# Gated mix of 16-head attention and a spectral filter on one core: larger VectorE instructions, zero-column folds, and squares and small products moved between VectorE and GpSimd

## The chip, the cores and the metric

The kernel runs on one NeuronCore of a Trainium2 chip. The metric is the device time of one execution in microseconds (us). Instructions run on five in-order engines: TensorE (PE in the profile), ScalarE (ACT), VectorE (DVE), GpSimd (POOL) and SyncE (SP, which only issues DMAs). An engine works through its own instructions in the order in which they stand, and waits for the others through semaphores.

## The reference

One input `x` (2048 rows of 448, bf16) goes two ways, and a gate per row mixes them:

```
g = sigmoid((x * gate_w).sum(-1))
q, k, v = split(x @ wqkv, 16 heads of 28)
a = softmax(q @ k^T / sqrt(28)) @ v, heads joined, @ wo
b = irfft2(rfft2(x) * (w_r + 1j * w_i))          # over rows and columns
out = g * a + (1 - g) * b
```

## The kernel before

**Attention.** The heads go in 4 groups of 4 (`g`), the queries in 4 chunks of 512 (`qc`), so there are 16 chunks `c = 4 g + qc`. A chunk has 64 units of scores: 16 key tiles of 128 by 4 heads, each unit a matmul into 128 x 512 floats of PSUM (`scores`, L1143). A unit becomes weights in one of two ways. On ACT, an `exp` takes two units at once out of a two-bank buffer `psA` (L1166, 128 x 1024); there are two such buffers, and PE fills one while ACT reads the other. On DVE, a "z" step takes one unit out of a bank `psX` and builds the bits of the power of two by an integer addition (L1188, 128 x 512); it then needs two "shift" copies per pair of units (L1208, 128 x 1024 integers), on DVE or POOL, and PE multiplies three results with the values instead of one. PE adds up weights times values in one bank `psV` (`values`, L1227). At a chunk's end DVE copies `psV` to `Oraw` (L363, the helper `copy_to`), and a chain normalises it: row sums to DRAM and back, a reciprocal (L1283), the product with the gate's odds (`n4`, L1284, on DVE), a broadcast through DRAM, and a product on POOL (L1291).

**Projections.** Keys and queries of group g are projected (L351, the helper for all column-tiled matmuls), evicted by DVE (L533, L590) and squared into `sqk` on POOL (L544, L594) for their norms. Values are projected once for heads 0 to 3 in the head of the program, and for heads 4 to 15 in 16 pieces of 336 columns (`vproj`), each evicted by one DVE instruction (L363, `V<-psX`).

**The spectral branch** runs beside the attention. POOL folds `x` into sums and differences of columns d and 448-d (L720), leaving columns 0 and 224 to small copies (L722). PE applies the transforms; DVE evicts `AT` (L736) and `bufB` (L743). In the middle, for each of 16 groups of frequencies, PE makes the spectrum; DVE multiplies its 450 columns by the real and by the imaginary filter, one instruction each (L767, `T<-psX,Wst`); POOL combines them (L773, L775); PE transforms back, and DVE evicts two pieces of 113 and 112 rows (`vt_evict`, L816). At the end DVE evicts each of 16 row tiles (L800), and POOL unfolds it in three instructions (L805, L807, and L809 for two columns).

**Output.** For each of 16 row tiles t, PE adds four head groups times `wo` and the spectral part in one bank; DVE (L855) or, for the last four tiles, ACT (L857) scales it into one of four buffers `fin` (`fin_154` to `fin_157`, tile t into buffer t mod 4), and a DMA writes it out. Tile t waits until the DMA of tile t-4 has read the buffer. The last four tiles wait for the last chunk: `finale` (L1326) transposes, divides and transposes back `psV` in two halves on DVE (L1336 to L1345), after which PE adds each tile's last product.

**The order** of all this is not written by hand. Every step is an `Op` with a fixed cost per engine, and `plan()` runs a list scheduler over them before anything is emitted; the numbers in `TUNE` set due times and thresholds. `want_D` decides for each group of units how many take the DVE way, from the work it counts as waiting on DVE and POOL. Steps marked `port` are kept by the planner from running on DVE and POOL at the same time, and for shifts a dependency is added when the order is emitted, so that POOL's next step waits for DVE's:

```
if o.port and e == "DVE" and self.free_at["POOL"] > t + self.PW and t - o.at < self.PT:
    continue
...
if o.eng == "DVE" and o.kind == "shift":
    port = r
elif o.eng == "POOL" and port is not None and r is not None:
    self.tc.add_manual_dep(r.ins, port.ins.name, mybir.DependencyInfo(
        mybir.DependencyClass.Sync, mybir.DependencyReason.DATA), reason="common port")
```

Of the kernel before, what the change touches and what calls it, by code (L numbers as in the profile page):

```python
# [47 lines left out]
def constants():  # L48
    c = {}
    p = np.arange(128)  # L50
    small = np.zeros((128, 1152))
# [18 lines left out]
    small[:, 992:1120] = -C1.T  # L70
# [13 lines left out]
    for ch, (d0, lo) in enumerate(((0, 0), (HF - 1, 1), (1, 0), (HF - 2, 3))):  # L84
        dd = (d0 + np.arange(HF))[:, None]
        Bd[lo:HF, ch] = (np.cos if ch < 2 else lambda v: -np.sin(v))(2 * np.pi * dd * f / D)[lo:]
    c["Bd"] = Bd
# [6 lines left out]
    Bv = np.zeros((128, 2, D))  # L94
    for ch, (f0, fn) in enumerate(((0, 113), (113, 112))):
        Bv[:fn, ch, 0:F] = Br[f0:f0 + fn]
        Bv[:fn, ch, F:D] = Bi[f0:f0 + fn, 1:F - 1]
# [67 lines left out]
class Unit:  # L165
    __slots__ = ("bank",)

    def __init__(self):
# [3 lines left out]
TUNE = dict(T0=16487.535, LC=21704.657, late=6305.21, pzmin=4, urg=6, lastd=3, dt1=1190.3066700269546, dt2=962.0521051112778,  # L172
            minx2=1, poolt=4891.347115056346, th=141.972, pw=216.675, pt=2570.424, ph=426.68181980690866, slack=208.898,
            q0a=0.7, q0b=0.859, q0n=1.2209003708584167, v0=0.7381326711175313, v1=0.16, vr=0.293, kb=-3.0, ks=0.25, kn=-2.285,
            qb=-1.4867786877722318, qs=0.2435943825577399, qn=-1.89, gate=0.725, fo=1.497, fos=0.457, fa=4.071245811511132,
            fas=0.29, sp=3.653, sps=4811.435849142648, fc=7.428, fcs=0.272, fp=11.902, fps=0.165, fsd=46632.287,
            ow=12161.038102559343, ows=1062.607, u8=743.705, u12=13562.139, relx=10124.439740798462, comb=0, mc=28.681)
# [14 lines left out]
class Kernel:  # L192
    def __init__(self, tc, A_x, A_wqkv, A_wo, B_w_r, B_w_i, gate_w, out):
        self.tc = tc
        self.nc = tc.nc
        self.x, self.wqkv, self.wo = A_x, A_wqkv, A_wo
        self.w_r, self.w_i, self.gate_w = B_w_r, B_w_i, gate_w
        self.out = out
        self.ops = []
        self.NP = 24  # L200
        self.COMB = TUNE["comb"]

# [23 lines left out]
    def emit_all(self):  # L226

        port = None
        for o in sorted(self.order, key=lambda o: (o.start, o.num)):
# [3 lines left out]
            if o.eng == "DVE" and o.kind == "shift":  # L233
# [6 lines left out]
    def tiles(self):  # L240
# [4 lines left out]
        self.small = T([128, 1152], BF16, "small")  # L245
# [11 lines left out]
        self.Wv = self.Wst[0:112, 8 * D:12 * D].rearrange("p (c n) -> p c n", c=4)  # L257
# [6 lines left out]
        self.Bv = self.Bst[:, 0:2 * D].rearrange("p (c d) -> p c d", c=2)  # L264
# [9 lines left out]
        self.XF = vt[:, 0:NT * D].rearrange("p (t d) -> p t d", t=NT)  # L274
# [35 lines left out]
        self.C1N = self.small[:, 992:1120]  # L310
# [50 lines left out]
    def copy_to(self, eng, out, in_):  # L361
        if eng == "DVE":
            self.nc.vector.tensor_copy(out=out, in_=in_)  # L363
        elif eng == "POOL":
            self.nc.gpsimd.tensor_copy(out=out, in_=in_)
        else:
            self.nc.scalar.copy(out=out, in_=in_)  # L367

    def head(self):
# [3 lines left out]
        self.vd, self.kb_d, self.nq_d = [], {}, {}  # L373
# [6 lines left out]
        d_small = self.dma("small", lambda: dict(out=self.small[:], in_=self.cst["small"].ap()), 288, prio=H0 + 1.5)  # L380
# [13 lines left out]
        w_v = self.dma("Wv", lambda: dict(out=self.Wv, in_=wv[:, :, 2 * D:3 * D]), 400, prio=H0 + 6, rows=448)  # L394
# [42 lines left out]
        self.d_wv, self.d_gw = [w_v], d_gw  # L437
# [79 lines left out]
    def kproj(self, g, prio, prio_n, head):  # L517
# [3 lines left out]
        for b in range(4):  # L521
# [20 lines left out]
            else:  # L542
                e1 = self.ev(f"ke{g}{b}", {"DVE": 665.0}, fin, [p, self.d_f32] + old, pb, u=u)
                e2 = self.ev(f"ks{g}{b}", {"POOL": 1120.0}, lambda e, b=b: nc.gpsimd.tensor_tensor(  # L544
                    out=self.sqk[:, QW * b:QW * b + QW], in0=self.kT[g][:, QW * b:QW * b + QW],
                    in1=self.kT[g][:, QW * b:QW * b + QW], op=ALU.mult), [e1] + ([self.nq_d[g - 1]] if g else []), pb)
# [849 lines left out]
```

## Time and profile before

| | |
|---|---|
| three runs | 385.93, 385.90, 385.18 us (median 385.9) |
| profiled execution, its own time | 385.22 us |
| its span, first to last instruction | 383.4 us |
| busy in the span | PE 360.7, ACT 363.3, DVE 331.3, POOL 257.4 us |
| ACT's exps | 384 of 404 instructions, 353.8 us |
| DVE's z steps and shifts | 257 and 117 instructions, 171.0 and 49.8 us |
| granted TensorE clock | 0.999 |

In the profile a row reads: line, engine, operation, output<-input (partitions x elements, type) xcount | busy us, mean ns of one | idle time just before, and what ended it. Busy time is a union: where one instruction starts before the last has been reported ended, the mean times the count is more than the busy time. The span is 1.8 us shorter than the execution's time; what lies outside belongs to the start and end of a launch.

### The profile page before, as it was taken

The page shows a single profiled execution, that of the slowest core. Times are in us where ns is not written, and L with a number is a line of the kernel's source. Part 1 is how long each engine was busy: PE and PEld are TensorE (multiplying, and loading weights), DVE is VectorE, ACT ScalarE, POOL GpSimd, SP SyncE. Part 2 cuts the span into 40 slices and gives each one's busy share as a digit, 9 for nine tenths or more (in the row PEclk, how much of TensorE's full clock was granted, in tenths as well). Part 3 has the DMA queues.
Part 4 walks back from the last instruction along what each step waited for, and adds up shares of the span by engine and source line. Part 5 has one row for each costly group of instructions (what it writes and reads, how often), then busy time and mean ns, then how long its engine had stood idle before and what let it go on. Part 6 is the DMA issues. An engine that isn't in the chain of part 4 may idle for free.

```text
span 383.4 us, 13098 instructions
## 1 busy us (share of the span) xinstructions
PE 360.7 (94%) x5374; PEld 133.0 (35%) x5374; DVE 331.3 (86%) x636; ACT 363.3 (95%) x404; POOL 257.4 (67%) x292
## 2 busy tenths in 40 slices
PE   6999999999999999899999999999999989899994
PEld 5453233333233333333333433333333333232232
DVE  0567987986999999999999999999999899989962
ACT  3899999999999999999999999999999999999952
POOL 4327778778657676667757866667767666677692
PEclk9999999999999999999999999999999999999999
DMA  7700012201123312344122421312000000111012
GB/s 207 193 3 3 4 5 36 41 2 30 29 42 70 75 39 42 89 50 90 43 55 59 127 65 27 93 29 52 5 11 24 20 13 3 31 38 41 26 50 76
DMA packets 42869, 18.60 MB, mean 49 GB/s; under 512 B 28932, under 2 KB 40828, under 8 KB 42808
## 3 DMA queue, kind: packets, MB, share of 16 engines
q1 hardware_dynamic: 42808, 17.75, 21.1%
q8 instruction: 42, 0.69, 0.9%
q14 instruction: 19, 0.16, 0.2%
HBM read 13.77 MB, written 2.07 MB: 41 GB/s over the span
## 4 chain that ended last, share of the span: by engine, by line
PE 53%; ACT 29%; DVE 11%; issue 5%; DMA 2%; DVEq 0%; ACTq 0%
ACT P L1166 29%; PE psA L1143 19%; PE psX L351 16%; PE psV L1227 14%; DVE P L1188 5%; PE psX L403 1%; DMA out_dram<-fin 1%; DVE P L1208 1%; DVE AT L736 1%; PE psA L351 1%; PE psX L449 1%; DVE bufB L743 1%; PE psV L351 1%; DVE fin L855 1%; DVE bufB L800 0%
## 5 line engine op out<-in xcount | busy, mean ns | idle before, releaser
L1166 ACT ACTIVATE P<-psA 128x1024 bf16<-128x1024 f32 x384 | 353.8, 1139 | 1.3 <-PE psA L1143 0.7
L1208 POOL TENSOR_SCALAR P<-P 128x1024 int16<-128x1024 int16 x143 | 148.4, 1038 | 69.5 <-DVE P L1208 26.1
L1188 DVE TENSOR_SCALAR P<-psX 128x512 int16<-128x512 f32 x257 | 171.0, 683 | 17.3 <-PE psX L1143 14.6
L1143 PE MATMUL psA<-qT,kT 32*128 32x512 bf16 x767 | 149.0, 382 | 10.6 <-ACT P L1166 8.4
L1227 PE MATMUL psV<-P,V 128*32 128x512 bf16 x1538 | 132.7, 384 | 0.1
L1143 PE MATMUL psX<-qT,kT 32*128 32x512 bf16 x257 | 92.4, 385 | 0.0
L1143 PEld LDWEIGHTS <-kT 32*128 32x128 bf16 x1024 | 45.1, 91 | 134.9 <-issue 130.1
L1208 DVE TENSOR_SCALAR P<-P 128x1024 int16<-128x1024 int16 (+1 forms) x117 | 49.8, 429 | 0.5
L1227 PEld LDWEIGHTS <-V 128*32 128x32 bf16 x1538 | 33.3, 95 | 46.1 <-issue 41.7
L351 PE MATMUL psX<-xT,Wp 112*32 112x512 bf16 x512 | 40.4, 384 | 1.2 <-ACT Wp L367 1.2
L1291 POOL TENSOR_TENSOR qT<-Oraw,Rbc 128x512 bf16<-128x512 f32 x14 | 17.8, 1272 | 6.4 <-DVE P L1208 6.2
L594 POOL TENSOR_TENSOR sqk<-qT 128x512 bf16<-128x512 bf16 x14 | 14.5, 1039 | 6.3 <-DVE P L1208 5.9
L767 DVE TENSOR_TENSOR T<-psX,Wst 128x450 bf16<-128x450 f32 x32 | 18.7, 614 | 0.0
L351 PE MATMUL psX<-Wst,xT 112*32 112x336 bf16 (+1 forms) x384 | 16.9, 278 | 0.0
L720 POOL TENSOR_TENSOR VT<-bufA 128x892 bf16<-128x892 bf16 x8 | 14.2, 1776 | 2.7 <-DVE P L1208 2.5
L351 PEld LDWEIGHTS <-Wp 112*32 112x32 bf16 x512 | 10.2, 95 | 15.7 <-issue 13.6
L544 POOL TENSOR_TENSOR sqk<-kT 128x512 bf16<-128x512 bf16 x12 | 12.5, 1040 | 3.8 <-DVE P L1208 2.4
L351 PEld LDWEIGHTS <-VT 128*32 128x32 bf16 (+3 forms) x512 | 10.4, 95 | 10.2 <-issue 8.8
L773 POOL TENSOR_TENSOR bufA<-T 128x225 bf16<-128x225 bf16 x16 | 9.0, 560 | 6.5 <-DVE T L767 4.1
L816 DVE CAST VT<-psX 113x256 bf16<-113x256 f32 (+1 forms) x32 | 11.9, 414 | 0.5 <-PE psX L351 0.3
L351 PE MATMUL psX<-Bst,VT 113*32 113x225 bf16 (+3 forms) x256 | 11.7, 264 | 0.3 <-DVE VT L816 0.3
L805 POOL TENSOR_TENSOR bufA<-bufB 128x223 bf16<-128x223 bf16 x16 | 9.7, 609 | 3.4 <-DVE P L1208 3.2
(100 smaller groups left out, 290.0 us busy)
## 6 DMA issues: line engine op xcount, KB each, us to landing
Rbc<-dR SPq DMA_DIRECT2D x14, 256.0 KB
IV<-c_IV SPq DMA_DIRECT2D x16, 128.0 KB
bufA<-bufB SPq DMA_DIRECT2D x16, 112.5 KB
bufA<-in_A_x_dram SPq DMA_DIRECT2D x4, 448.0 KB
out_dram<-fin SPq DMA_DIRECT2D x16, 112.0 KB
S<-c_S SPq DMA_DIRECT2D x16, 96.0 KB
Wst<-in_B_w_r_dram SPq DMA_DIRECT2D x7, 112.5 KB
Wst<-in_B_w_i_dram SPq DMA_DIRECT2D x7, 112.5 KB
```

What stands on the lines that cost most here:

```text
L351: self.nc.tensor.matmul(o[c:c + n], lhsT=w[:, c:c + n], rhs=r, start=start, stop=stop, tile_position=(0, c), skip_group_check=True)
L544: e2 = self.ev(f"ks{g}{b}", {"POOL": 1120.0}, lambda e, b=b: nc.gpsimd.tensor_tensor(out=self.sqk[:, QW * b:QW * b + QW], in0=self.kT[g][: ...
L594: sq.append(self.ev(f"qs{g}{qc}", {"POOL": 1120.0}, lambda e, qc=qc: nc.gpsimd.tensor_tensor(out=self.sqk[:, QW * qc:QW * qc + QW], in0=se ...
L720: fs.append(self.ev(f"fo{tg}{k}", {"POOL": 1860.0}, lambda e, ts=ts, k=k, op=op, lo=lo, hi=hi: nc.gpsimd.tensor_tensor(out=self.XF[:, ts, ...
L767: es.append(self.ev(f"fm{g}{ri}", {"DVE": t_dve(F2)}, lambda e, u=u, T=T, g=g, ri=ri: nc.vector.tensor_tensor(out=T[:, ri, :].rearrange("p ...
L816: self.nc.vector.tensor_copy(out=self.VT[0:fn, ch, :, :, 8 * g:8 * g + 8], in_=u2.bank[0:fn, 256 * ch:256 * ch + 256].rearrange("p (r t k) ...
L1143: nc.tensor.matmul(out, lhsT=self.kT[g][32 * j:32 * j + 32, 128 * kt:128 * kt + 128], rhs=self.qT[g][qc][32 * j:32 * j + 32, :], start=Tru ...
L1166: e = self.op("exp", {"ACT": t_act(QW * n)}, lambda o: self.nc.scalar.activation(out=self.P[slot][:, 0:n, :], in_=self.PSA[i][:, 0:n, :], ...
L1188: e = self.op("z", {"DVE": t_dve(QW)}, lambda o: self.nc.vector.tensor_scalar(out=zt.bitcast(I16), in0=ub.bank, scalar1=float(ZBASE), scal ...
L1208: return en.tensor_scalar(out=self.P[q[1 + s]][:, 0:n, :].bitcast(I16), in0=self.P[q[0]][:, 0:n, :].bitcast(I16), scalar1=1.0, scalar2=flo ...
L1227: self.nc.tensor.matmul(self.PSV[32 * j:32 * j + 32, :], lhsT=self.V[:, kt, 4 * (i // NQ) + j, :], rhs=rhs, start=first, stop=False, tile_ ...
L1291: n = self.ev(f"n7_{c}", {"POOL": 1350.0}, lambda e: nc.gpsimd.tensor_tensor(out=self.qT[g][qc][:], in0=self.Oraw[r][:], in1=self.Rbc[r][: ...
```

## The change

The spectrum product becomes one instruction per group over 900 columns (both filters), and the middle eviction one of 512 columns over 113 rows (the second piece now begins one row earlier, at 112, with that row's weight zero). The values of heads 4 to 15 are projected in 4 pieces of 4 row tiles x 112 columns (heads 4 to 7) and 8 pieces of 2 row tiles x 224 columns (heads 8 to 15), whose weights are now loaded in two halves, the second into a free part of the tile `VT`. The fold works on 225 columns, with a zero column appended, so that its small copies go; the unfold loses its two-column copy in the same way. Squares may run on DVE or POOL; both shifts of a pair may run on either; `n4` goes to POOL. The ordering rule for `port` steps now covers every such step of DVE. All numbers in `TUNE` are new.

```diff
-            es = []
-            for ri in range(2):
-                es.append(self.ev(f"fm{g}{ri}", {"DVE": t_dve(F2)}, lambda ...: nc.vector.tensor_tensor(
-                    out=T[:, ri, :]..., in0=u.bank[:, 0:F2]..., in1=self.Wsp[:, g:g + 1, ri, :].to_broadcast([128, 2, F]), ...
+            e = self.ev(f"fm{g}", {"DVE": t_dve(2 * F2)}, lambda ...: nc.vector.tensor_tensor(
+                out=T[:].rearrange("p r (a f) -> p r a f", a=2),
+                in0=u.bank[:, 0:F2]....to_broadcast([128, 2, 2, F]),
+                in1=self.Wsp[:, g, :, :]....to_broadcast([128, 2, 2, F]), op=ALU.mult),
...
     def vt_evict(self, u2, g):
-        for ch, fn in ((0, 113), (1, 112)):
-            self.nc.vector.tensor_copy(
-                out=self.VT[0:fn, ch, :, :, 8 * g:8 * g + 8],
-                in_=u2.bank[0:fn, 256 * ch:256 * ch + 256]...)
+        self.nc.vector.tensor_copy(
+            out=self.VT[:, :, :, :, 8 * g:8 * g + 8].rearrange("p c r t k -> p (c r t) k"),
+            in_=u2.bank[0:HF, :].rearrange("p (m k) -> p m k", k=8))
...
+    def square(self, name, out, x, deps, prio):
+        o = self.ev(name, {"POOL": 1120.0, "DVE": 340.0}, lambda e: (self.nc.vector if e == "DVE" else self.nc.gpsimd).tensor_tensor(
+            out=out, in0=x, in1=x, op=ALU.mult), deps, prio)
+        o.port = True
...
-            so = self.op("shift", {"DVE": 70.0 + 0.265 * QW * n, "POOL": 110.0 + 1.05 * QW * n}
-                         if s == 0 else {"POOL": 110.0 + 1.05 * QW * n}, emit, prev, -1e7)
+            so = self.op("shift", {"DVE": 70.0 + 0.265 * QW * n, "POOL": 110.0 + 1.05 * QW * n}, emit, prev, -1e7)
...
-        r2 = self.ev(f"n4_{c}", {"DVE": 165.0}, lambda e: nc.vector.tensor_tensor(
+        r2 = self.ev(f"n4_{c}", {"POOL": 190.0}, lambda e: nc.gpsimd.tensor_tensor(
...
-            if o.eng == "DVE" and o.kind == "shift":
+            if o.eng == "DVE" and o.port:
...
-        for t in range(NT):
-            self.vproj(t, at(w["v0"] + w["v1"] * t), at(w["vr"] + 0.1 * t))
+        self.vd1 = [self.vproj(b, 4, ...) for b in range(4)]
+        self.vd2 = [self.vproj(b, 2, ...) for b in range(8)]
...
-            lo, hi = self.bufA[:, ts, 1:F - 1], self.bufA[:, ts, D - 1:F - 1:-1]
+            lo, hi = self.bufA[:, ts, 0:F], self.bufA[:, ts, D:F - 2:-1]
...
-TUNE = dict(..., poolt=4891.347115056346, ..., pt=2570.424, ..., v0=0.7381326711175313, ..., u8=743.705, u12=13562.139, ...)
+TUNE = dict(..., poolt=7236.982, ..., pt=5990.959, ..., v0=1.5, ..., va=4.36, ..., u8=-4013.039, u12=20639.587, ...)
```

The new order differs throughout. Counted over the whole of each engine's order, ACT has 383 exps of 1024 columns and one of 512 before, and 382 of 1024 now; DVE has 257 z steps, 117 shifts and no square before, and 260, 113 and 18 now; POOL has 143 shifts and 26 squares before, and 155 and 8 now; PE has 1538 matmuls of weights times values before, and 1544 now; its value projections for heads 4 to 15 are 256 matmuls of 336 columns before, and 256 of 112 and 256 of 224 columns now, each with a weight load. Three places follow.

DVE in the spectral middle: `T` is the spectrum product, `VT` the middle eviction, `P` from `psX` a z step, `P` from `P` a shift. Before:

```order
L767 TENSOR_TENSOR T_1_129<-psX_163,Wst 128x450 x2
L816 CAST VT<-psX_162 113x32x8
L816 CAST VT<-psX_162 112x32x8
L767 TENSOR_TENSOR T_0_128<-psX_161,Wst 128x450 x2
L816 CAST VT<-psX_163 113x32x8
L816 CAST VT<-psX_163 112x32x8
```

and now:

```order
L815 CAST VT<-psX_162 113x64x8
L1179 TENSOR_SCALAR P_103<-psX_161 128x512
L770 TENSOR_TENSOR T_0_128<-psX_163,Wst 128x900
L1179 TENSOR_SCALAR P_105<-psX_162 128x512
L1199 TENSOR_SCALAR P_96<-P_103 128x1024
L538 TENSOR_SCALAR kT_74<-psX_161,f32c 128x512
L1199 TENSOR_SCALAR P_100<-P_105 128x512
L368 TENSOR_TENSOR sqk<-kT_74 128x512
```

Four instructions per group have become two, they stand between z steps and no longer in one block, and a square of the keys has come in.

DVE at the end of the program: `psV` is read by the first transposes of `finale`, `fin` are the output tiles (here t = 9, 10, 11 in buffers 155, 156, 157). Before:

```order
L1336 STREAM_TRANSPOSE psX_162<-psV 128x256
L1338 RECIPROCAL Rsm_136<-psX_161 128x8
L1338 RECIPROCAL Rsm_137<-psX_162 128x8
L1340 TENSOR_TENSOR Rsm_136<-Rsm_136,oddsT 128x8
L855 TENSOR_SCALAR fin_155<-psA_159,omg 128x448
L1340 TENSOR_TENSOR Rsm_137<-Rsm_137,oddsT 128x8
L1342 TENSOR_TENSOR nq_92<-psX_161,Rsm_136 128x256
L1342 TENSOR_TENSOR nq_93<-psX_162,Rsm_137 128x256
L1345 STREAM_TRANSPOSE qT_3_90<-nq_92 128x256
L1345 STREAM_TRANSPOSE qT_3_90<-nq_93 128x256
L855 TENSOR_SCALAR fin_156<-psA_159,omg 128x448
L855 TENSOR_SCALAR fin_157<-psA_160,omg 128x448
```

and now:

```order
L846 TENSOR_SCALAR fin_155<-psX_161,omg 128x448
L1327 STREAM_TRANSPOSE psX_163<-psV 128x256
L1327 STREAM_TRANSPOSE psA_159<-psV 128x256
L1329 RECIPROCAL Rsm_136<-psX_163 128x8
L846 TENSOR_SCALAR fin_156<-psA_159,omg 128x448
L1329 RECIPROCAL Rsm_137<-psA_159 128x8
L1331 TENSOR_TENSOR Rsm_136<-Rsm_136,oddsT 128x8
L846 TENSOR_SCALAR fin_157<-psA_160,omg 128x448
L1331 TENSOR_TENSOR Rsm_137<-Rsm_137,oddsT 128x8
L1333 TENSOR_TENSOR nq_92<-psX_163,Rsm_136 128x256
L1333 TENSOR_TENSOR nq_93<-psA_159,Rsm_137 128x256
L1336 STREAM_TRANSPOSE qT_3_90<-nq_92 128x256
```

Tile 9 has moved ahead of the transposes, and tiles 10 and 11 from behind the whole chain into it. On PE, tile 9's products have moved ahead of the last multiplication with the values.

ACT at its end: the last exps, then output tiles 12 to 15. Before:

```order
L1166 ACTIVATE P_112<-psA_159 128x1024
L1166 ACTIVATE P_95<-psA_160 128x512
L857 ACTIVATE fin_154<-psA_160,omg 128x448
L857 ACTIVATE fin_155<-psX_163,omg 128x448
L857 ACTIVATE fin_156<-psA_159,omg 128x448
L857 ACTIVATE fin_157<-psA_159,omg 128x448
```

and now:

```order
L1157 ACTIVATE P_103<-psA_159 128x1024
L1157 ACTIVATE P_112<-psA_160 128x1024
L848 ACTIVATE fin_154<-psA_160,omg 128x448
L848 ACTIVATE fin_156<-psX_161,omg 128x448
L848 ACTIVATE fin_157<-psA_159,omg 128x448
```

The last exp is a whole one now, and tile 13 has gone to DVE.

160 lines of the change are left out of this document (74 added, 86 removed).

## Prediction

> **What bounds the kernel now.** I read the page's busy times and groups first, then busy times by stage, then the waits, and last the timeline of the end. From the page:
>
> ```profile
> PE 360.7 (94%) x5374; PEld 133.0 (35%) x5374; DVE 331.3 (86%) x636; ACT 363.3 (95%) x404; POOL 257.4 (67%) x292
> L1166 ACT ACTIVATE P<-psA 128x1024 bf16<-128x1024 f32 x384 | 353.8, 1139 | 1.3 <-PE psA L1143 0.7
> L1188 DVE TENSOR_SCALAR P<-psX 128x512 int16<-128x512 f32 x257 | 171.0, 683 | 17.3 <-PE psX L1143 14.6
> ```
>
> PE and ACT look alike at 94 and 95%. The second row tells them apart: ACT stood idle ahead of its 384 exps for 1.3 us in all. A matmul's reported time overlaps the next one's, so PE's share says less. An exp costs ACT 353.8 / 384 = 0.92 us (its reported 1139 ns overlaps the next). The busy times by stage, where the stages are the head, the first chunks, the middle, the last chunks, and what follows the last product with the values:
>
> ```profile
> 13.30:33.00 19.70, 19.11 (x492) 10.14 (x491) 12.53 (x22) 18.94 (x24) 7.61 (x12) 1.00 0.18 46
> 33.00:96.00 63.00, 63.00 (x864) 19.41 (x863) 50.89 (x97) 63.00 (x71) 49.35 (x45) 1.00 0.14 18
> 96.00:336.00 240.00, 228.95 (x3345) 82.01 (x3343) 231.97 (x451) 239.49 (x262) 164.30 (x180) 1.00 0.22 47
> 336.00:370.60 34.60, 33.53 (x440) 10.33 (x440) 28.53 (x53) 33.98 (x38) 25.87 (x36) 1.00 0.12 37
> 370.60:383.40 12.80, 7.14 (x138) 3.93 (x130) 5.15 (x14) 2.53 (x4) 5.81 (x15) 0.96 0.23 74
> ```
>
> The columns after the stage and its length are PE, its weight loads, DVE, ACT, POOL, the granted clock and the DMAs. From 33 to 370 us ACT is busy 336.5 of 337.6 us: the time of this stretch is the number of exps times 0.92. DVE has 8.0 us free of 240 in the middle, PE 11.0. The last stage is different: 12.8 us in which nobody is busy half the time except PE, a chain. In the timeline of its engines (start, length):
>
> ```profile
> 369.97 0.68 DVE L855 TENSOR_SCALAR fin<-psX,omg 128x448 bf16<-128x448 f32 x1 [0.95 <-PE psX L351]
> 370.64 0.80 DVE L1336 STREAM_TRANSPOSE psX<-psV 128x256 f32<-128x256 f32 x2
> 371.99 0.68 DVE L855 TENSOR_SCALAR fin<-psA,omg 128x448 bf16<-128x448 f32 x1
> 372.73 0.94 PE L351 MATMUL psA<-Wo,qT 128*32 128x448 bf16 x16 [0.84 <-DVE fin L855]
> 373.79 0.76 DVE L1345 STREAM_TRANSPOSE qT<-nq 128x256 bf16<-128x256 bf16 x2
> 374.48 0.64 DVE L855 TENSOR_SCALAR fin<-psA,omg 128x448 bf16<-128x448 f32 x1
> 375.29 0.68 DVE L855 TENSOR_SCALAR fin<-psA,omg 128x448 bf16<-128x448 f32 x1 [0.18 <-issue]
> 376.00 3.97 DMA out_dram<-fin
> 376.45 0.63 ACT L857 ACTIVATE fin<-psA,omg 128x448 bf16<-128x448 f32 x1 [6.46 <-PE psA L351]
> 377.40 0.63 ACT L857 ACTIVATE fin<-psX,omg 128x448 bf16<-128x448 f32 x1 [0.31 <-PE psX L351]
> 378.34 0.63 ACT L857 ACTIVATE fin<-psA,omg 128x448 bf16<-128x448 f32 x1 [0.31 <-PE psA L351]
> 379.03 0.37 PE L351 MATMUL psA<-Wo,qT 128*32 128x448 bf16 x4 [0.73 <-ACT fin L857]
> 380.06 0.63 ACT L857 ACTIVATE fin<-psA,omg 128x448 bf16<-128x448 f32 x1 [1.08 <-DMA out_dram<-fin]
> ```
>
> (The row of the DMA is from the chain that ended last.) The division of the last chunk ends at 374.55. But tile 11 is scaled only at 375.29, behind it; its buffer comes free 3.97 us later; tile 15, which uses that buffer, is scaled at 380.06 and is the end. PE, too, waited twice: 0.84 us for a bank that tile 9 held, 0.73 us for one that ACT held.
>
> **The change, part by part.** The sum is made against the profiled execution, 385.2 us, which stands 0.7 below the median of the runs, 385.9.
>
> *Exps.* Of the 1024 units, 260 instead of 257 take the DVE way. 764 units are 382 full exps, 767 were 383.5: 1.5 x 0.92 = **1.4 us less** on the engine that bounds 33 to 370 us. ACT's other steps are the same there and in the head.
>
> *DVE.* The rows by form, one with two neighbours for a price:
>
> ```profile
> L767 DVE TENSOR_TENSOR T<-psX,Wst 128x450 bf16<-128x450 f32 x32 | 18.7, 614 | 0.0
> L816 DVE CAST VT<-psX 113x256 bf16<-113x256 f32 (+1 forms) x32 | 11.9, 414 | 0.5 <-PE psX L351 0.3
> L736 DVE CAST AT<-psX 113x512 bf16<-113x512 f32 x16 | 10.8, 675 | 0.0
> L363 DVE CAST V<-psX 128x336 bf16<-128x336 f32 x16 | 8.0, 503 | 3.2 <-PE psX L351 3.2
> L363 DVE COPY xT<-psX 112x1024 bf16<-112x1024 bf16 x5 | 3.4, 687 | 8.9 <-PE psX L449 8.8
> L1284 DVE TENSOR_TENSOR Rsm<-Rsm,odds x14: 158/171/919, 62.0 to 339.9; 128x16 f32<-128x16 f32 x14
> L1284 DVE TENSOR_TENSOR Rsm<-Rsm,odds 128x16 f32<-128x16 f32 x14 | 5.6, 398 | 0.0
> L1208 DVE TENSOR_SCALAR P<-P x117: 284/417/695, 39.0 to 368.3; 128x1024 int16<-128x1024 int16 x114, 128x512 int16<-128x512 int16 x3
> L1311 DVE TENSOR_TENSOR nq<-Rbc,Rsm 128x512 bf16<-128x512 f32 x1 | 0.7, 691 | 0.0
> ```
>
> From 256 and 512 columns (414, 675 ns): 1.02 ns a column and 153 ns fixed. The product over 900 columns is then 1.07 us in place of 2 x 0.614, 16 times: -2.5. The eviction is 0.675 for 2 x 0.414: -2.45. The values: 12 x 0.61 for 16 x 0.503: -0.7. `n4` leaves: -5.6. Four shifts fewer at 0.43: -1.7; three z steps more: +2.05; tile 13: +0.7. The 18 squares, 512 bf16 columns with both inputs in SBUF, are not in the trace; the nearest rows are the shift (median 417 ns) and the product at 512 columns of floats (691). I take 417: the copy of 1024 bf16 columns costs 687, as 512 of floats do, so bf16 runs at twice the rate, and (675 - 153) / 2 + 153 = 414. +7.5, at most +12.4. Sum: 2.7 us less (2.2 more at the upper end), off the path while DVE's 8.0 us of idle time in the middle last. **0**.
>
> One rule speaks against the squares. The row of `n4` shows it first: the same instruction took 158 ns at best and 919 at worst. The Trainium skill says on its page GPSIMD Engine Reference, section 8, that POOL shares its SBUF interfaces with DVE, and that DVE instructions with two SBUF inputs contend with it. That would explain the 919, and a square has two such inputs. By the median rows the squares cost 7.5 us; if each waited as long as the worst `n4`, 18 x (0.691 + 0.748) = 25.9. I stay with the first, since the order keeps squares apart from POOL's steps as it does shifts, whose worst is 695; the second is a rival below.
>
> *POOL.* From
>
> ```profile
> L594 POOL TENSOR_TENSOR sqk<-qT 128x512 bf16<-128x512 bf16 x14 | 14.5, 1039 | 6.3 <-DVE P L1208 5.9
> L1208 POOL TENSOR_SCALAR P<-P 128x1024 int16<-128x1024 int16 x140 | 146.6, 1047 | 69.3 <-DVE P L1208 26.1 <-DVE P L1188 15.0 <-PE psX L1143 7.8
> L809 POOL COPY bufA<-bufB 128x2 bf16<-128x2 bf16 x16 | 3.1, 194 | 3.8 <-DVE P L1208 2.1 <-PE psX L351 0.8 <-PE psX L1143 0.4
> L722 POOL COPY VT<-bufA 128x8 bf16<-128x8 bf16 x4 | 0.9, 224 | 2.4 <-DVE P L1208 2.4
> L679 POOL CAST V<-wk 128x64 bf16<-128x64 f32 x1 | 0.5, 471 | 9.3 <-ACT wk L513 9.3
> ```
>
> 18 squares fewer (-18.7), 12 shifts more (+12.5), the small copies gone (-4.0 with those of the fold), 14 `n4` more at 0.19 to 0.47 each (+2.7 to +6.6). POOL gains 4 to 8 us of 257 and has 76 us free in the middle: **0**. `n4` now queues behind a shift, so up to 1.05 us later, and behind it SP's `dR` transfer with all that SP holds after that; the chain ends in a product that only the output reads, in the last group of heads. The added waits (POOL behind squares as behind shifts) cost POOL at most 18 x 0.8 (26.1 us over 33 waits now): 14 of its 76.
>
> *PE.* Six more products with the values, in sets of four, and value projections in twice as many instructions. The rows
>
> ```profile
> L351 PE MATMUL psX<-Wst,xT 112*32 112x336 bf16 x256 | 14.5, 310 | 0.0
> L351 PE MATMUL psX<-Wst,xT 112*32 112x112 bf16 x128 | 2.5, 213 | 0.0
> PE psA L1143 <- ACT P L1166: 8.4, 30, 0.5
> ```
>
> show 0.43 ns a column; 112 + 224 columns stream as long as 336. The 64 additional sets cost what is not per column: for 112 columns 2.5 us / 32 sets = 0.078, less 0.048: 0.03 each, 1.9 us; at the lower end nothing. It lies where PE waits for ACT (8.4 us). **0**, 1 to 2 if that cover is gone. The second half of the weights comes in one more DMA in the head, ahead of `Bd`, which nothing needs before the transforms. The first middle eviction now waits for the last value projection, as the order has it, just ahead of it on DVE; before, 16 of these evictions stood in a row without z steps between, and ACT was busy all the same.
>
> *The end.* Tile 9's scaling now stands ahead of the transposes: they start 0.6 us later. The chain from transposes to transposes took 370.64 to 374.55, 3.9 us, with one output tile in it; with two it is 4.6. So the division ends 0.6 + 0.1 + 4.6 = 5.3 us after the last product with the values, in place of 4.0. What follows is shorter. PE has 30 sets left in place of 35 and no bank to wait for; 22 of them (0.19 each, 4.2 us) are done before the division ends. Then one product (0.4 with its start), three ACT steps at the 0.95 us of the rows 376.45 to 378.34 (tile 13 goes beside them on DVE), so ACT ends at 5.3 + 0.5 + 2 x 0.95 + 0.63 = 8.3, or 7.7 if back to back. From ACT's end, 380.69, to the span's end are 2.7 us: 11.0 or 10.4 in place of 12.8. Tile 11 leaves DVE at about 3.9; even with 3.97 us of landing its buffer is free at 7.9, and the end at 11.2. So **2.0 us less**, between 1.6 and 2.4; 0 if the buffer or the chain holds it as now. That tile 9's five sets stand ahead of the last product hides behind the last two exps (1.8 us); without that it costs 1.0.
>
> 385.2 - 1.4 - 2.0 = 381.8. For a median I add a third of the 0.7 by which the profiled execution is low: **382.0**.
>
> **Rivals.** *The end gives nothing back* (a late output buffer, as now): 385.2 - 1.4 = 383.8. For it: the 3.97 us landing, which can fall on another tile. Against: three tiles now go out earlier. Chance 0.2.
>
> *PE holds ACT up where the values of heads 8 to 15 are now projected* (about 95 to 180 us). Two thirds of 64 x 0.145 = 9.3 us, 6.2, come into 85 us that have 11.0 / 240 of it free, 3.9: up to 2.3 late, 384.1, unless the transforms that start earlier make room. Chance 0.12.
>
> *DVE becomes the bound through the squares*, slower than before. DVE's 8.0 idle us and the 2.7 gained last until the squares cost 18.2 us, 1.0 each; every us beyond is a us of the kernel, and from 1.24 us each it is slower than before. At 1.44 each it is 7.7 over: 389.5. For it: POOL is busy 68% of the middle, and the 919 ns. Against: the median of 171 beside it. Chance 0.12.
>
> **How the numbers follow.** The forecast has 0.56. A run of this kernel can be told from no change beyond 0.2%, 0.8 us. Forecast, the first rival and most of the second lie below 385.1: 0.80, less what is unknown of stalls in a new order, 0.78. Slower: 0.16, the rest 0.06. The range goes from the end's best (2.4) with another us of luck, 380.4, to just short of no gain at all, 385.0; the third rival is left out.
>
> **What would show it.** Right: 382 exps at 0.92 us with little idle time ahead of them, squares near 0.42 us, the last ACT step 8 us after the last product with the values. Wrong: squares over 1 us, or exps that wait for PE between 95 and 180 us, or a last tile that waits for its buffer.

## Result and profile after

The changed kernel takes 382.25 us (median of 6, 380.70 to 383.48), the kernel before 385.55 (6, 385.13 to 385.93): ratio 0.9913, 95% interval 0.9888 to 0.9939. Forecast were 382.0 and faster. The sum came out; one of its two terms is hardly to be seen in the profile after, and the reason is worth more than the hit, which is in part luck (below).

The profiled execution of the changed kernel took 382.98 us, span 380.9. From the page, and from the groups by form:

```profile
PE 360.1 (95%) x5636; PEld 136.1 (36%) x5636; DVE 330.6 (87%) x604; ACT 360.5 (95%) x401; POOL 247.6 (65%) x281
L1157 ACT ACTIVATE P<-psA 128x1024 bf16<-128x1024 f32 x382 | 351.8, 1152 | 3.2 <-PE psX L1134 2.0 <-PE psA L1134 1.1
L770 DVE TENSOR_TENSOR T<-psX,Wst 128x900 bf16<-128x900 f32 x16 | 17.4, 1088 | 0.2 <-PE psX L350 0.2
L815 DVE CAST VT<-psX 113x512 bf16<-113x512 f32 x16 | 10.9, 680 | 1.9 <-PE psX L350 1.9
L362 DVE CAST V<-psX 128x448 bf16<-128x448 f32 x12 | 7.4, 618 | 0.5 <-PE psX L350 0.4
L368 DVE TENSOR_TENSOR sqk<-qT x10: 409/418/443, 43.3 to 269.8; 128x512 bf16<-128x512 bf16 x10
L368 DVE TENSOR_TENSOR sqk<-kT x8: 409/419/718, 52.1 to 236.1; 128x512 bf16<-128x512 bf16 x8
L1274 POOL TENSOR_TENSOR Rsm<-Rsm,odds x14: 215/216/217, 64.4 to 340.0; 128x16 f32<-128x16 f32 x14
```

382 exps, as counted; but ACT stood idle 3.2 us ahead of them where it was 1.3. The prices were right: product 1.088 us (1.07 forecast), eviction 0.680 (0.675), values 0.618 (0.61), squares 0.418 (0.417), `n4` on POOL 0.216 (0.19 to 0.47).

Cut where the exps begin and end, the two profiles differ so:

```
                                    before    after   difference
start to first exp                   13.48    12.94    -0.54
first exp's start to last one's end 356.50   356.37    -0.13
last exp's end to end of span        13.45    11.57    -1.88
```

The end gave what was forecast. The stretch of the exps, 1.5 of them shorter, did not move. Busy times of the changed kernel around its longest waits (columns as in the prediction, the granted clock third from the right):

```profile
300.00:302.00 2.00, 1.98 (x43) 0.75 (x33) 1.71 (x4) 2.00 (x4) 1.46 (x2) 1.00 0.29 81
302.00:304.00 2.00, 1.31 (x17) 0.45 (x13) 1.99 (x5) 2.00 (x4) 1.15 (x3) 1.00 0.15 58
304.00:306.00 2.00, 1.68 (x18) 0.58 (x17) 2.00 (x5) 2.00 (x3) 1.18 (x3) 1.00 0.00 0
306.00:308.00 2.00, 1.96 (x25) 0.71 (x26) 2.00 (x6) 2.00 (x3) 1.27 (x3) 0.58 0.03 8
308.00:310.00 2.00, 2.00 (x18) 0.24 (x10) 0.44 (x1) 1.13 (x2) 1.25 (x2) 0.50 0.14 4
310.00:312.00 2.00, 2.00 (x19) 0.44 (x17) 1.05 (x2) 1.40 (x2) 0.00 (x0) 0.50 0.00 0
312.00:314.00 2.00, 1.89 (x17) 0.38 (x13) 1.64 (x4) 1.63 (x2) 1.04 (x2) 0.71 0.00 0
```

From 306.3 to 313.1 us the granted clock is 0.5: PE is full and ACT waits. In the 4 us from 302 PE started 17 and 18 matmuls in 2 us, where it was 43 in the 2 us from 300. Not every execution has this: the mean clock of the six was 0.991, 0.994, 0.996, 0.999, 1.000 and 1.000. So below I also give means over the executions with a clock of 0.998 or more. Of the runs of before beside the experiments these are 42 of 57, and take 385.0 us. Of the 18 executions of the changed kernel and of two variants of it that have its order on PE and ACT up to 369 us they are 7, and take 381.3; the other 11 take 382.8. **The change is worth 3.7 us where the clock holds, and loses 1.5 of it in most executions.**

The end (timeline of its engines):

```profile
369.85 0.39 PE L1216 MATMUL psV<-P,V 128*32 128x512 bf16 x4
370.67 0.46 DVE L1327 STREAM_TRANSPOSE psX<-psV 128x256 f32<-128x256 f32 x1
371.81 0.68 DVE L846 TENSOR_SCALAR fin<-psA,omg 128x448 bf16<-128x448 f32 x1
372.62 0.68 DVE L846 TENSOR_SCALAR fin<-psA,omg 128x448 bf16<-128x448 f32 x1
373.35 0.56 PE L350 MATMUL psA<-Wo,qT 128*32 128x448 bf16 x8 [0.85 <-DVE fin L846]
373.96 0.76 DVE L1336 STREAM_TRANSPOSE qT<-nq 128x256 bf16<-128x256 bf16 x2
375.24 0.38 PE L350 MATMUL psA<-Wo,qT 128*32 128x448 bf16 x4
375.67 0.63 ACT L848 ACTIVATE fin<-psA,omg 128x448 bf16<-128x448 f32 x1 [6.36 <-PE psA L350]
377.13 0.63 ACT L848 ACTIVATE fin<-psA,omg 128x448 bf16<-128x448 f32 x1 [0.31 <-DMA out_dram<-fin]
```

Three ACT steps instead of four; the last ends 7.5 us after the last product with the values (370.24), where it was 10.1 (from 370.56 to 380.69).

### The profile page after: what moved, and what is told of

It reads as the page before. It is cut to its first block, busy times and chain, and to the rows that moved or that the text cites. A ratio compares the mean times of both kernels' runs of the same rounds, so it can differ in the third digit from the quotient of the medians.

```text
span 380.9 us, 13544 instructions
## 1 busy us (share of the span) xinstructions
PE 360.1 (95%) x5636; PEld 136.1 (36%) x5636; DVE 330.6 (87%) x604; ACT 360.5 (95%) x401; POOL 247.6 (65%) x281
## 4 chain that ended last, share of the span: by engine, by line
PE 60%; ACT 28%; DVE 5%; issue 4%; DMA 1%; ACTq 0%; DVEq 0%
ACT P L1157 27%; PE psA L1134 22%; PE psX L350 19%; PE psV L1216 16%; DVE P L1179 3%; PE psX L408 1%; DMA out_dram<-fin 1%; DVE P L1199 1%; PE psA L350 1%; ACT xT L365 1%; DVE VT L815 0%; DMA ident<-c_small 0%; PE psV L350 0%; PE psX L1134 0%; DVE T L770 0%
## 5 line engine op out<-in xcount | busy, mean ns | idle before, releaser
L1199 POOL TENSOR_SCALAR P<-P 128x1024 int16<-128x1024 int16 (+1 forms) x155 | 158.6, 1024 | 73.5 <-DVE P L1179 24.6
L1134 PE MATMUL psX<-qT,kT 32*128 32x512 bf16 x260 | 88.6, 387 | 0.0
L770 DVE TENSOR_TENSOR T<-psX,Wst 128x900 bf16<-128x900 f32 x16 | 17.4, 1088 | 0.2 <-PE psX L350 0.2
L350 PEld LDWEIGHTS <-Wp 112*32 112x32 bf16 x512 | 10.6, 94 | 15.7 <-issue 13.6
L350 PEld LDWEIGHTS <-xT 112*32 112x32 bf16 x768 | 12.8, 96 | 8.3 <-issue 7.3
L727 POOL TENSOR_TENSOR VT<-bufA 128x900 bf16<-128x900 bf16 x8 | 14.3, 1791 | 1.5 <-DVE P L1199 0.9
L350 PE MATMUL psX<-Wo,qT 128*32 128x448 bf16 x192 | 14.2, 356 | 0.0
L350 PEld LDWEIGHTS <-VT 113*32 113x32 bf16 (+2 forms) x512 | 9.9, 95 | 7.9 <-issue 6.8
L815 DVE CAST VT<-psX 113x512 bf16<-113x512 f32 x16 | 10.9, 680 | 1.9 <-PE psX L350 1.9
L778 POOL TENSOR_TENSOR bufA<-T 128x225 bf16<-128x225 bf16 x16 | 9.8, 613 | 4.1 <-DVE P L1199 4.0
L776 POOL TENSOR_TENSOR bufA<-T 128x225 bf16<-128x225 bf16 x16 | 9.0, 560 | 5.2 <-DVE P L1199 3.1
L846 DVE TENSOR_SCALAR fin<-psX,omg 128x448 bf16<-128x448 f32 x11 | 7.5, 678 | 5.1 <-PE psX L350 5.1
```

The source lines that it names most:

```text
L350: self.nc.tensor.matmul(o[c:c + n], lhsT=w[:, c:c + n], rhs=r, start=start, stop=stop, tile_position=(0, c), skip_group_check=True)
L727: fs.append(self.ev(f"fo{tg}{k}", {"POOL": 1860.0}, lambda e, ts=ts, k=k, op=op, lo=lo, hi=hi: nc.gpsimd.tensor_tensor(out=self.XF[:, ts, ...
L770: e = self.ev(f"fm{g}", {"DVE": t_dve(2 * F2)}, lambda e, u=u, T=T, g=g: nc.vector.tensor_tensor(out=T[:].rearrange("p r (a f) -> p r a f" ...
L778: y2 = self.ev(f"fz{g}", {"POOL": 580.0}, lambda e, T=T, g=g: nc.gpsimd.tensor_tensor(out=self.bufA[:, g, F:F2], in0=T[:, 1, 0:F], in1=T[: ...
L815: self.nc.vector.tensor_copy(out=self.VT[:, :, :, :, 8 * g:8 * g + 8].rearrange("p c r t k -> p (c r t) k"), in_=u2.bank[0:HF, :].rearrang ...
L1134: nc.tensor.matmul(out, lhsT=self.kT[g][32 * j:32 * j + 32, 128 * kt:128 * kt + 128], rhs=self.qT[g][qc][32 * j:32 * j + 32, :], start=Tru ...
```

## Experiments

In the tables and texts "idle" of 20 exps is the time from the first one's start to the 21st's, less 20 x 0.9045 us (the median between two starts is 0.904), worked out from their starts in the traces. (The 384 or 382 exps are cut at the same counts, so the columns of before and after stand for slightly different work. In the rows left out each variant lies within 0.21 us of the changed kernel.)

```
exps from   before  after  own   fill  fill1  sq2  sqpool  v2x
   0         3.25   3.85   5.74  3.77  4.36   3.74  3.96   3.77
  20         0.37   0.33   0.33  0.33  0.33   0.79  0.99   0.33
  40         0.23   0.26   0.26  0.26  0.26   1.67  1.84   0.26
 100         0.01   0.20   0.19  0.19  0.19   0.20  0.19   1.38
 120         0.35   0.35   0.36  0.36  0.36   0.35  0.36   0.82
 140         0.77   0.15   0.15  0.15  0.15   0.38  0.15   1.88
 160         0.40   0.36   0.35  0.35  0.36   0.76  0.94   1.24
 180         0.37   0.07   0.06   0.07   0.06   0.06  0.05   0.77
 220         0.50   0.27   0.27   0.27   0.27   0.76  0.27   0.27
 240         0.11   0.24   0.24  0.84  0.40   0.21  0.24   0.24
 300         0.37   2.60   0.38  0.77  0.55   0.38  0.38   0.39
```

**Output buffers (first rival).** In both kernels (before_own, after_own):

```diff
-        f = self.fin[t % 4]
+        f = self.bufB[:, t, 0:D]
```

> The kernel before, in which each output tile is scaled into its own slice of bufB (free by then) in place of one of four fin buffers; no instruction is moved. In the profile of before the last scaling on ACT began at 380.06 us after waiting 1.08 us for an output transfer, while its product, issued at 379.03, ended at 379.40. My reading: without that wait it begins about 0.2 us after the product, so the kernel gains 0.3 to 0.5 us: 385.1. The first rival (the end is set by late output buffers): the buffer accounts for the whole difference at the end, so 1.5 to 2 us: 383.6 to 384.0.

Measured 385.52 (12), 1.001 of before (0.9994 to 1.0026): nothing. ACT at the end of before_own:

```profile
376.98 0.64 ACT L857 ACTIVATE bufB<-psA,omg 128x448 bf16<-128x448 f32 x1 [6.94 <-PE psA L351]
380.02 0.64 ACT L857 ACTIVATE bufB<-psA,omg 128x448 bf16<-128x448 f32 x1 [0.52 <-PE psA L351]
```

From the first scaling on ACT to the last it is 3.04 us in place of 3.61: 0.57 is what the late buffer cost. The first comes 0.53 later, for in this variant a scaling on DVE waits 2.1 us for POOL steps on `bufB`; so the two cancel in the time. Either way the buffer does not make the 1.5 to 2 us of the rival.

> The changed kernel with the same edit, no instruction moved. In its profile the last scaling waited 0.31 us for an output transfer. My reading: 0 to 0.3 us less, 382.0 to 382.2; the first rival: 1 us or more, at most 381.2. All that runs before 369 us is the same program as the changed kernel, so this profile is also a second look at the stream of exps: by my count of 382 exps at 0.904 us each, it lasts about 355.2 us from the first exp's start to the last one's end where the granted clock stays at 1.0 (356.4 in the first profile, with a stretch of 6.8 us at 0.5); if the added steps cost the stream something everywhere, it lasts 356.4 again without such a stretch.

Measured 382.34 (6), 0.9926 of before (0.9904 to 0.9947), 381.4 in the three executions with full clock: no gain. The last scaling no longer waits for a transfer (0.17 us for PE instead of 0.31). Its profile has the half clock at another place, from 29.6 to 33.0 us, and not at 306: idle 5.74 in the first row of the table, 0.38 in the last. So the 2.2 us at 306 are not in the order, and without either stretch the exps last 356.09 - 1.97 = 354.1 us, less than the 355.2 that I expected; 356.37 - 2.2 gives 354.2 as well. Just ahead of that stretch PE was not short of matmuls, it started 182 in 4 us:

```profile
26.00:30.00 4.00, 3.33 (x182) 2.36 (x174) 1.94 (x6) 3.40 (x6) 0.03 (x1) 0.94 0.02 4
```

**Is the clock due to a sparse PE?** Products repeated into the same bank (after_fill; `num` counts the pairs of scores; after_fill1 repeats once):

```diff
+            more = 2 * mms[2:3] if 243 <= num <= 246 or 313 <= num <= 316 else []
-            for (c, kt, j), out in mms:
+            for (c, kt, j), out in mms + more:
```

> The changed kernel with 12 score products repeated into their own bank (two repeats each, the result is the same), at the six places near 240 and 303 us that have such a product and where TensorE had the fewest matmuls in 3.4 us (20 and 21 started, where the sparsest such stretch of before had 25). Theory: the stretch at a granted clock of 0.5 from 306 to 313 us follows from TensorE having little to do just before, and comes in some executions only. Then the mean granted clock is 0.999 or more in all runs (it was 0.991 to 1.000 in six of the changed kernel), the times lie within 1 us, and the median is 381.0 to 381.6. Rival: the clock falls whatever TensorE does there; then some runs show 0.99 again and the median is 382.0 to 382.7.

Measured 382.41, 0.9934 of before (0.992 to 0.9948). The clock was 0.998 to 1.000 in all six, the times 381.83 to 382.50. The theory's clock came, its median not: the repeats themselves hold the exps up, 0.6 us near 240 and 0.4 near 300 (table).

> The changed kernel with the score products near 240 and 303 us repeated once instead of twice (six repeats in place of twelve). Two repeats kept the granted clock at 0.998 and more in all six runs, but delayed exps: in 20 exps from 237 us the idle time ahead of them rose from 0.24 to 0.84 us, in those from 292 us from 0.39 to 0.77. One repeat should cost half of that, 0.5 us. If it is still enough to keep the clock up: all runs at 0.997 or more, 381.2 to 382.0. If it is not: some runs near 0.991 as in the changed kernel, and a median of 382.2 to 383.

Measured 381.16 (4, 380.85 to 382.14), 0.9889 of before (0.9865 to 0.9913), clock 0.998 to 1.000. The same place as above, in its profile:

```profile
304.00:306.00 2.00, 1.53 (x15) 0.43 (x14) 1.81 (x5) 2.00 (x4) 1.15 (x2) 1.00 0.07 28
306.00:308.00 2.00, 1.85 (x28) 0.62 (x22) 2.00 (x6) 1.93 (x3) 1.15 (x2) 1.00 0.02 4
308.00:310.00 2.00, 1.92 (x32) 0.62 (x24) 2.00 (x5) 2.00 (x4) 1.55 (x2) 1.00 0.01 4
```

Ten of ten executions with repeats stayed at 0.998 or more, 7 of 18 without them. That is weaker evidence than it looks: of the four other variants below that keep the sparse places (sq2, sqpool, v2x, l3) 27 of 41 executions stayed there with no repeats, and the repeats stand nowhere near the stretch at 29.6 us. The 2 us from 304 are even sparser here than where the clock fell; what exactly is counted stays open. This is the lowest median measured, but its interval overlaps the changed kernel's: beyond its steady clock no gain is shown.

**The larger instructions alone** (after_split): product and eviction issued as two instructions each, at the same places.

```diff
-                out=T[:]..., in0=...to_broadcast([128, 2, 2, F]), ...
+                out=T[:, ri, :]..., in0=u.bank[:, 0:F2]..., ... for ri in range(2)
...
+        for ch in range(2):
+            ...tensor_copy(out=self.VT[:, ch, :, :, 8 * g:8 * g + 8], in_=u2.bank[0:HF, 256 * ch:256 * ch + 256]...)
```

> The changed kernel with the spectrum product again as two instructions of 450 columns and the middle eviction again as two of 256 columns; what runs before and after them on each engine is unchanged. By the rows of before and after this is 16 x (2 x 0.614 - 1.088) = 2.2 us and 16 x (2 x 0.414 - 0.680) = 2.4 us more on DVE, which idles 26 us of the 335 from 33 to 368 us. My theory (DVE does not set the time; its larger instructions buy nothing by themselves): 0 to 0.5 us more than the changed kernel, 382.3 to 382.9. Rival (the larger instructions on DVE are where the gain is from): 2 to 4.6 us more, 384.3 to 387.

Measured 382.52, 0.9927 of before (0.9903 to 0.9952). Its profile has the half clock at 306.1 to 312.9 as well, and the exps last 356.46 us beside 356.37. The split cost nothing. It was a smaller dose than I expected, though: DVE's busy time rose from 330.6 to 332.6 us, by 1.9 and not by 4.6, since neighbouring instructions overlap by some 0.08 us, which the rows' means count twice.

**Squares.** Twice on DVE (after_sq2), or all 18 on POOL (after_sqpool), the order otherwise unchanged:

```diff
+ after_sq2:    the same tensor_tensor issued for i in range(2 if e == "DVE" else 1)
+ after_sqpool: lambda e: self.nc.gpsimd.tensor_tensor(out=out, in0=x, in1=x, op=ALU.mult)
+               if o.eng == "DVE" and o.port and o.kind != "sq":     # no POOL step waits for a square on DVE
```

> The changed kernel with each of the 18 squares issued twice on DVE, no other instruction moved: 18 x 0.41 = 7.4 us more on DVE, and POOL's next step waits behind the second square as well. My theory: most of it falls into DVE's idle time, so 0 to 1.5 us more than the changed kernel, 382.3 to 383.8. The third rival of the prediction (DVE is close to the bound, and two-input steps in SBUF hold POOL up): 4 to 7.4 us more, 386.3 to 389.7.

> The changed kernel with its 18 squares issued on POOL, at the same places of the order: DVE has 7.4 us less, POOL 18.7 us more. By the prediction's ledger POOL has some 76 us free there and DVE is off the path, so the engine does not matter: 382.0 to 382.6. Rival, from doubled squares (7.4 us more on DVE cost 2 to 3 us, most of it between 34 and 70 us where POOL's shifts waited for them): what counts is how long POOL's shifts stand behind a square, 1.04 us in place of 0.41, so 1 to 4 us more than the changed kernel, 383.3 to 386.3.

Measured 384.44 (12 runs, 0.9992 of before, 0.9974 to 1.001) and 384.55 (11 runs, 0.9979, 0.9963 to 0.9995); at full clock 384.3 and 384.3 beside 381.3: **3.0 us each**. So in this order the squares' place on DVE is worth most of the change's 3.7. My number for the first was too low, the third rival's too high; for the second the rival was right, and the ledger wrong. Busy times of the changed kernel, of after_sq2 and of after_sqpool, in this order, for the stretch of the first squares:

```profile
34.00:75.00 41.00, 40.68 (x714) 14.35 (x710) 38.88 (x73) 41.00 (x48) 30.28 (x26) 1.00 0.19 25
```

```profile
34.00:75.00 41.00, 40.12 (x677) 13.66 (x673) 39.41 (x75) 39.94 (x45) 29.18 (x25) 1.00 0.18 22
```

```profile
34.00:75.00 41.00, 39.50 (x644) 13.34 (x643) 38.56 (x66) 39.50 (x45) 34.22 (x31) 1.00 0.17 20
```

ACT loses 1.1 and 1.5 us there while DVE and POOL both have time left: 1.6 and 11.8 us free with doubled squares. So it is not the sum of an engine's work. I read it as a queue: a shift stands behind a square for 0.4 us more, or 0.6 where POOL does the square, and the products with the values behind the shift. POOL's waits that a square ended rose from 6.6 us in the changed kernel to 13.1 with doubled squares, which bears out the first half; the profiles name no wait of PE for a shift, so the second is argued. The square itself stays at its price in the median, 424 ns even when doubled.

The squares that took longer, up to 0.718 us in the changed kernel and 0.893 doubled, show what holds them. One of them, with the POOL step beside it:

```profile
51.48 1.04 POOL L1199 TENSOR_SCALAR P<-P 128x1024 int16<-128x1024 int16 x1 [1.21 <-PE psX L1134]
52.07 0.72 DVE L368 TENSOR_TENSOR sqk<-kT 128x512 bf16<-128x512 bf16 x1
```

The shift on POOL ends at 52.52, the square 0.27 later. It is so in every such case (ns, by the time that POOL was busy beside the DVE step; those between 100 and 150 ns left out):

```
                                 under 100 ns       150 ns or more
                                 count, length      count, length, length less POOL's time beside it
square, changed kernel and sq2   45, 408 to 427       7, 443 to 893, 269 to 282
shift, before                    89, 363 to 430      15, 440 to 695, 278 to 284
n4, before                        5, 158 to 166       6, 258 to 919,  19 to 31
z step, before                   14, 673 to 692     241, 628 to 693, no constant
```

The three steps that read SBUF alone end a fixed time after the POOL instruction beside them; the z step, which reads PSUM, takes as long either way. The squares are cheap since the order, in which POOL waits behind them, leaves 15 of the 18 under 100 ns beside POOL. What they cost without that ordering rule was not tried.

**PE's cover (second rival)** (after_v2x): the value projections of heads 8 to 15 computed twice.

```diff
+        for k in range(3, 8, 4) if n == 2 else ():
+            mms[k] = (..., lambda fs=[...the four products again...]: [f() for f in fs])
```

> The changed kernel in which the value projections of heads 8 to 15 are computed twice, the second time into the same bank with the same result: 256 more matmul instructions on PE (64 sets of four) between 109 and 187 us, no other engine's work changed. A set costs PE 224 x 0.43 / 1000 + 0.03 = 0.126 us at my rates, 8 us in all; PE has 1.3 us left in which it waits for nothing from 95 to 180 us in the profile of the changed kernel (3.95 in before). Theory (the second rival's cover was real, and the change has used it up to the last 1.3 us): the exps now wait for PE there, and the kernel takes 4 to 7 us more, 386 to 389. Rival (PE's busy time overstates its load, the cover is larger): 0 to 2 us more, 382.3 to 384.3.

Measured 385.91 (12), 1.0035 of before (1.0009 to 1.006), just below my 386 to 389; 385.8 at full clock, 4.4 more than the changed kernel. From 104 to 208 us, first the changed kernel, then this one:

```profile
104.00:208.00 104.00, 101.43 (x1574) 37.55 (x1566) 96.87 (x174) 104.00 (x115) 74.41 (x80) 1.00 0.30 58
```

```profile
104.00:208.00 104.00, 101.99 (x1769) 40.45 (x1766) 93.57 (x165) 101.01 (x109) 71.67 (x76) 1.00 0.29 57
```

ACT is busy all 104 us in the changed kernel; here it loses 3. The table has the loss in the rows from 100 to 180 (5.0 us) and nowhere else. The second rival named a real limit; the change stopped short of it. Of the 8 us that I reckoned for the doubling 4.4 came through, so by these rates some 3.6 us of cover were left and not 1.3.

**What an exp costs** (after_noz8): no unit of chunk 8 goes the DVE way.

```diff
-        if len(us) < n + 3 or us[-1][0] != c or (c == NQ * NG - 1 and kt >= NK - self.LASTD):
+        if len(us) < n + 3 or us[-1][0] != c or (c == NQ * NG - 1 and kt >= NK - self.LASTD) or c == 8:
```

> The changed kernel in which no unit of chunk 8 goes the DVE way: 387 full exps and a half instead of 382, 11 z steps fewer on DVE, and the order after chunk 7 planned anew. My theory (between 33 and 369 us each exp costs its 0.904 us): 5.5 x 0.904 = 5.0 us more than the changed kernel, 387.3, within 1 us for the new order. Rival (the time is set as much by DVE, PE and the waits between them, so exps for z steps is an even trade): 0 to 2 us more, 382.3 to 384.3.

Three executions with a clock of 0.995 to 0.997 took 388.0, 389.4 and 389.6 (1.0097 of before, 1.0065 to 1.0128); the other four, at 0.951 to 0.970, 395.9 to 400.0. So 6.7 us or more above the changed kernel's 381.3, in place of 5.0. The profile (an execution of 400.0 us) shows where the rest lies:

```profile
208.00:240.00 32.00, 31.40 (x252) 7.03 (x251) 14.48 (x22) 24.77 (x26) 9.52 (x13) 0.52 0.19 49
```

For 30.7 us the clock stayed at 0.5 although PE was busy 31.4 of the 32, and ACT was idle for 7 of them. In the three groups of 20 exps that hold its stretches at half clock (from 200, 220 and 340) the idle time is 11.7 us more than in after_own. Without these the exps last 370.8 - 11.7 = 359.1 us, 5.0 more than 354.1: the price of an exp is right. The end is not the same here: from the last product with the values to the end of the span it is 12.5 us in place of 10.6. These 1.9 us, from the order planned anew, and the 5.0 account for the 6.7 of the fastest execution, which at a clock of 0.997 has no room for a stretch of 3.41 us at half clock.

**The end's order** (after_l3): `lastd=3`.

> The changed kernel with lastd = 3 in place of 2: no unit of the last three key tiles of the last chunk goes the DVE way. The order differs from the changed kernel's only at the very end: half an exp more, two output tiles instead of one scaled ahead of the transposes, one instead of two within the division, and all partial sums of the last four tiles stand ahead of the division's end, with their last products together behind it. My reading: +0.46 us of exps, the last scaling 0.8 us earlier after the last product with the values: 381.9. If the exps alone counted: 382.7. If a tile ahead of the transposes costs its 0.6 us in full and nothing comes back: 383.3.

Measured 382.57, 0.9944 of before (0.9925 to 0.9962), 382.3 at full clock: 0.9 more than the changed kernel. Half an exp is 0.45; the end is 11.2 us from the last product with the values (368.51) in place of 10.6. (The median is close to my 382.7 for the exps alone, but not for its reason.) DVE's last transposes and PE's last groups in its profile:

```profile
371.82 0.76 DVE L1336 STREAM_TRANSPOSE qT<-nq 128x256 bf16<-128x256 bf16 x2
373.69 0.94 PE L350 MATMUL psA<-Wo,qT 128*32 128x448 bf16 x16
374.68 0.63 ACT L848 ACTIVATE fin<-psA,omg 128x448 bf16<-128x448 f32 x1 [7.03 <-PE psA L350]
```

The division ends at 372.58, but PE is still at partial sums until about 374.1 (two sets of the group at 373.69), the fourth tile's among them. So the first scaling on ACT comes 6.2 us after the last product with the values, where the changed kernel needs 5.4. My 0.8 us of gain took PE to be done with them by then; here it is PE that sets the pace of the end. Which of the moved tiles brings the end's gain over before was not tried one by one.

**Code and numbers apart** (before_newnum, after_oldnum): each kernel with the other's `TUNE`, all but the keys of the value projections.

> The kernel before with the planner's numbers of the changed kernel (all but those of the value projections, which mean something else in the two). It sends 255 units the DVE way: 384.5 exps in place of 383.5, and leaves four output tiles' last products in an order near the changed kernel's. By my terms: 0.9 us more for exps, 1 to 2 us less at the end: 0.1 to 1.1 us less than before, so 384.2 to 385.2. Rival (the new numbers are the gain, whatever the code): 3 us less than before, 382.3.

> The code of the changed kernel with the planner's numbers of before (those of the value projections are the new ones). It sends 246 units the DVE way: 389 exps, 7 more than the changed kernel and 5.5 more than before. By my terms 7 x 0.904 = 6.3 us more than the changed kernel for exps, the end within 1 us: 387.5 to 389.5, slower than before. Rival (the larger instructions and moved squares bring the time down by themselves): at most before's 385.3.

Measured 401.3 (1.0408 of before, 1.0369 to 1.0447) and 391.5 (1.016, 1.0122 to 1.0199). The second is 2 us above my range; it is 389.0 at its best (clock 0.994), within it, and all its executions had some half clock. The first is a miss by 16 us. Waits of ACT in before_newnum between 96 and 340 us (in total, times, the longest):

```profile
ACT P L1172 <- PE psA L1149: 8.8, 4, 7.6
ACT P L1172 <- POOL sqk L550: 2.3, 1, 2.3
```

Near 206 us exps waited 7.6 us at one stroke, where PE's own waits name POOL's shifts and squares; and four stretches at half clock, 27.3 us in all, took more. What each took of the 16 was not tried. Neither the code nor the numbers are an improvement alone.

## Why the prediction was right, and where it was not

*Exps, -1.4.* The count and the price are right (382; 0.904 us between starts in every profile). At full clock the stretch of the exps is 354.1 to 354.2 us, 2.3 less than before: 1.36 for 1.5 exps and 1.0 for fewer waits (idle from the 20th exp on: 6.1 us before; after, with the stretch at half clock counted as in after_own, 4.5), against 0.5 more ahead of the 20th, at 33 us. The step that failed is "the time of this stretch is the number of exps times 0.92": it holds only while PE's clock does. In the profiled execution the half clock cost 2.2 us, and -0.13 was left. That the median came within 0.3 us of 382.0 is luck in part: at full clock the exps gave 0.9 more than forecast, and the lower clock of most executions, which the prediction does not have, took about as much back.

*The end, -2.0.* Measured -1.9 from the last exp, -2.2 from the last product with the values (10.6 us instead of 12.9; 10.4 to 11.0 in the other profiles with this end). Inside, errors cancelled: the division ended 4.5 us after that product, not 5.3, since the transposes began 0.4 us after it instead of 0.7 and the chain took 4.05 instead of 4.6; but PE, having waited 0.85 us for a bank, started the last products 0.5 later than that; ACT ended at 7.5, ahead of both my 7.7 and my 8.3; and from there to the span's end it was 3.1, not 2.7.

*DVE and POOL, 0.* Right for the larger instructions (split again: nothing). Not right for the squares: with 6.9 us more on DVE by its busy time, or 18.0 more on POOL with 76 to spare, the kernel takes 3.0 us more. The ledger adds up busy and idle time over 240 us; what decided, as I read it, was a queue of a few steps. The ledger's size was off as well: it multiplies mean lengths that overlap, so DVE got 0.6 us less to do (331.3 to 330.6) and not 2.7.

*PE, 0.* Right, with a limit near: 0.1 to 0.4 us of idle time per 20 exps from 100 to 200; with the values of heads 8 to 15 computed twice the kernel takes 4.4 us more.

*Head.* Forecast as unchanged, 0.54 us earlier in the profile. That is not the change's: see below.

*Rivals.* The first is refuted by the end itself and by both variants with own buffers. The second's mechanism is real beyond the dose of this change. The third is refuted in its price (squares at 0.418 us, none near 1.0; worst 0.718), not in its mechanism. The rule of the Trainium skill that I cited for it (GPSIMD Engine Reference, section 8) would have made the squares slower where POOL works, and this trace agrees: a square beside a POOL step lasts until 0.27 us after that step's end, and the 919 ns of `n4` in before end 0.02 us after a POOL shift. What kept the squares cheap is the order, as the prediction said when it stayed with the median.

## What to carry to other kernels

Price an engine by its busiest queue of dependent steps and not by its idle total: 1.9 us more on DVE were free in one place, and 6.9 us cost 3.0 in another. Keep DVE's steps that read SBUF alone away from POOL's running instructions: here squares, shifts and `n4` waited for the end of one, up to 0.9 us. Look at TensorE's clock in every execution before explaining a difference of half a per cent, and read two profiles: a stretch at half clock in one of them can hide the whole gain. A schedule's numbers belong to its code; exchanging either alone cost 6 and 16 us.

## What the hardware did that I had not expected

TensorE's granted clock fell to 0.5 on one core, in the midst of work. The stretches in the profiles last 3.41, 6.83, 10.24 and 30.7 us, multiples of 3.41. The Trainium skill (TensorE: Matmul & The Clock Gate, Part 1) has a window of that length, free-running, and says that an idle one halves the clock and a busy one restores it. The length agrees, and that the window runs freely fits with executions that differ. The rest does not: the clock fell when PE was busy 3.0 of 4 us, and stayed at 0.5 for 30.7 us in which PE was busy 31.4 of 32. A small number of matmuls does not explain it either: the sparsest 3.4 us have 21 started in the changed kernel and 25 in before, but 20 in after_fill and after_fill1, whose clock held, and in after_own the clock fell at 29.6 us behind 4 us with 182. The cause stays open.

The same clock moves the head. In the six profiles where it rose to 1.0 by 6.2 us from the start (the changed kernel's among them) the first exp began at 12.9 to 13.1 us; in the eight where it rose between 7.0 and 8.5 (before's among them) at 13.5 to 13.7, variants of the changed kernel in both. The head's 0.54 us between the two first profiles is this, and no effect of the change.
